# Regrouping the W' matmuls into eight bursts, and spacing the one-hot bursts of a spectral/expert mix kernel

## The chip, the cores and the metric

The kernel runs on one core of a Trainium2 chip. The metric is the device time of one execution on that core, in microseconds (us). Before the change three runs gave 765.38 us as their median, the lowest 765.37 and the highest 766.67.

A core has five engines, each with an instruction stream of its own that it works through in order: TensorE (PE, matmuls, with weight loads shown apart as PEld), VectorE (DVE), ScalarE (ACT), GpSimd (POOL) and SyncE (SP, which here issues DMA loads). They meet at semaphores: an instruction that needs another engine's result carries a wait, and everything behind it on its own engine waits with it. TensorE writes to PSUM, eight banks of 2 KB per partition (512 columns of float32); ACT and DVE read results from there.

## The reference

The output mixes two layers, token by token, for 2048 tokens of width 640:

```python
g = sigmoid((x * gate_w).sum(-1, keepdims=True))
# A: Fourier mixing, real part of a 2-d DFT by matmuls
a = einsum("bsd,ed->bse", x, dft_hid_re);  b = einsum("bsd,ed->bse", x, dft_hid_im)
A = einsum("ts,bse->bte", dft_seq_re, a) - einsum("ts,bse->bte", dft_seq_im, b)
# B: product-key experts, 32 heads, 16 x 16 keys, 256 experts
q = einsum("nd,dhc->nhc", x, w_q)
s1, s2 = q[..., :128] @ k1.T, q[..., 128:] @ k2.T       # 16 scores each
# two best of s1, two best of s2, the best two of the four sums -> expert ids and softmax gates
out_B = sum over heads and the two picks of  gate * gelu(x . u[expert]) * v[expert]
return g * A + (1 - g) * out_B
```

Two parts matter here. The scores are linear in x, so `w_q` and the keys can be multiplied first: W' = w_q x keys is a 640 x 1024 matrix (64 half-heads of 16 keys), and the scores are x times W'. And the picks of each token become a 16 x 16 table per token, built as the product of two "one-hot" matrices (rows compared with 0..15), one small matmul per token.

## The kernel before, in words

All large matmuls are float32 products in three passes (`mm3`, lines 139 to 141): both operands are split into a high part (a copy on ACT, line 134) and a low part (a subtraction on DVE or POOL, line 135). Most of them belong to the Fourier layer along the sequence. That work is cut into 152 *pieces*: each piece is one 128 x 512 block of a DFT matrix, loaded over SP into one of the `wf` tiles, split into `WS`, and multiplied with the five 128-column blocks of `X`: 15 matmuls of 128x512 that accumulate in banks 0 to 4. Everything else is laid between the pieces. The order is written out by hand: `at(n, f)` puts a function behind piece `n`, `follow(n)` calls them, and each engine's stream holds what is called in just that order. From piece 31 on, a background queue (`Pump`) also feeds in work for DVE in proportion to the TensorE time that its own account has passed.

**W'.** W' is made during the first 31 pieces. `w_q` arrives in 32 quarter blocks of 640 KB (`load_wq`, a pool of `WQB` buffers `wq`, loaded on SP). One quarter is one `w_part`: four matmuls (line 529) with 32 weight columns each, which write the four 32-partition groups of one PSUM bank, columns 0 to 319. Four quarters make one group `G` of 128 rows of W': two banks (5 and 6, from `ps_s`), two quarters added up in each. ACT copies the finished halves to `wp` (line 535). Then `w_transposes` turns the group around: five 128x128 transposes on TensorE (line 541) into bank 7 (`ps_t`), a copy on ACT (the high part, line 543) and a subtraction on DVE (the low part, line 544). `bursts` says behind which piece this happens: 16 bursts of two quarters each, behind pieces 4, 6, 8, 10, 12, 14, 16, 17, 18, 19, 20, 22, 23, 24, 25 and 27, and two that hold transposes alone. Four transposes of a group stand at the head of one burst and the fifth at the head of the next. A quarter's buffer is loaded again as soon as its matmuls are done, so the SP stream waits for TensorE there.

During the first 13 pieces `split_x` (ACT and DVE) and `gate_sum` (DVE, line 458) of the incoming rows of x stand between the same pieces; behind piece 14, `gate` runs a sigmoid on ACT.

**One-hot bursts.** From 442 to 548 us of the profiled span, `experts` handles 32 blocks of 64 tokens, two to a group. `build` makes the two one-hot matrices on DVE (lines 877 to 881). `use` issues the group's 64 matmuls of 32x32 (line 908) into bank 7, and `sums` copies the bank to `cd` on ACT (line 889) and stores it. Bank 7 is the only one for this, so the next group's matmuls wait for that copy. A group is used when two more have been built; when the buffers run short, and at `bg.drain()` behind piece 134, all that is built is used at once.

Of the kernel before, what the change touches and what calls it, by code (L numbers as in the profile page):

```python
# [8 lines left out]
F32 = mybir.dt.float32  # L9
F32R = mybir.dt.float32r  # L10
F16 = mybir.dt.float16
AF = mybir.ActivationFunctionType
# [4 lines left out]
P = 128  # L17
# [11 lines left out]
KD = D // P  # L29
# [12 lines left out]
NPC = Q1 + NT  # L42
# [58 lines left out]
def gated_mix_kernel(ctx: ExitStack, tc: tile.TileContext, xT, xn, dreT, dimT, wsre, wsim, wq, kT, uT, vv, gw, out):  # L101
    nc = tc.nc
# [9 lines left out]
    def rotate(what, n):  # L112
        turn[what] = (turn.get(what, -1) + 1) % n
        return turn[what]

    def bank(n, shape=(P, TC), dt=F32):
        return psum.tile(list(shape), dt, name=f"b{n}", tag=f"b{n}")

    def ps_s(shape=(P, TC)):
        return bank(5 + rotate("pss", 2), shape)  # L120

    def ps_t(shape, dt=F32):
        return bank(7, shape, dt)
# [25 lines left out]
    bg = Pump()  # L149
# [5 lines left out]
    WU = [big.tile([P, 2, KD, TC], F32R, name="WU", tag=f"WU{a}") for a in range(2)]  # L155
# [62 lines left out]
    def at(n, f, *args):  # L218
        then.setdefault(n, []).append(lambda: f(*args))
# [259 lines left out]
    t = ps_t([P, 512])  # L479
# [14 lines left out]
    identf = const.tile([P, P], F32)  # L494
# [16 lines left out]
    at(6, fill_rest)  # L511

    wqs, wps, wp = {}, {}, {}
    WQB = 5
    NWQ = 4 * NG

    def load_wq(m):
        if m < NWQ:
            wqs[m] = p1.tile([P, 4, HALF], F32, name="wq", bufs=WQB)
            nc.sync.dma_start(wqs[m], wq[m])  # L520

    def w_part(m):
        G, r, n = m // 4, m // 2 % 2, m % 2
        if r == 0:
            wps[G, n] = ps_s()
        ps = wps[G, n]
        w = wqs.pop(m)
        for j in range(4):
            nc.tensor.matmul(ps[32 * j:32 * j + 32, :HALF], kp[:, 8 * G // H, r, :], w[:, j], start=(r == 0),  # L529
                             stop=(r == 1))  # L530
        load_wq(m + WQB)
        if r == 1:
            if n == 0:
                wp[G] = p1.tile([P, D], F32, name="wp", bufs=1)
            nc.scalar.activation(wp[G][:, n * HALF:(n + 1) * HALF], wps.pop((G, n))[:, :HALF], AF.Copy)  # L535

    def w_transposes(G, k0, k1):
        f = wp[G]
        t = ps_t([P, 4, P])
        for k in range(k0, k1):  # L540
            nc.tensor.transpose(t[:, k - k0, :], f[:, k * P:(k + 1) * P], identf)  # L541
        h, l = (WU[G // 4][:, n, k0:k1, P * (G % 4):P * (G % 4 + 1)] for n in range(2))
        nc.scalar.activation(h, t[:, :k1 - k0], AF.Copy)  # L543
        nc.vector.tensor_sub(l, t[:, :k1 - k0], h.bitcast(F32))  # L544

    uf = {}

# [27 lines left out]
    for n in range(NT - 2):  # L575
        at(n, gate_sum, n + 2)
    for m in range(WQB):
        at(m, load_wq, m)

    bursts = [4 + m if m < 14 else 17 + (m - 14) * 10 // 16 for m in range(0, NWQ, 2)]  # L580
    n = bursts[-1]
    bursts += [n + 1, n + 2]
    for j, b in enumerate(bursts):
        if j >= 2:
            at(b, w_transposes, j // 2 - 1, *((4, KD) if j % 2 else (0, 4)))
        if 2 * j < NWQ:
            at(b, w_part, 2 * j)
            at(b, w_part, 2 * j + 1)
    n += 3
    at(n - 8, load_xT, 0)  # L590
    for k in range(KD):
# [248 lines left out]
    for p in range(NP):  # L840
        n = N0 + 5 * p + p // 2
# [20 lines left out]
    def experts():  # L862


        cd = {}

        def build(g, c, s, n, us):
            shp = [P, 16 * n, E, 4]
            pt, qt = (HOT[s // 2][:, o, s % 2:s % 2 + n].rearrange("p a (m e t) -> p (a m) e t", e=E, t=4)
                      for o in range(2))  # L870

            def row(o):
                r = ROWS[g][:, o, 8 * c:8 * (c + n), :].rearrange("p b (s t) -> p (b s) t", t=4)
                return r[:, :, None, :].to_broadcast(shp)

            wt = wtab4[:, None].to_broadcast(shp)
            nc.vector.tensor_tensor(pt, row(0), wt, op=OP.is_equal)
            yield us
            nc.vector.tensor_tensor(qt, row(1), wt, op=OP.is_equal)
            yield us  # L880
            nc.vector.tensor_tensor(pt, pt, row(2), op=OP.mult)
            yield us

        def sums(g, c, t):
            n = t.shape[1]
            if c % 4 == 0:
                cd[0] = pa.tile([P, E, 2, 4 * 8], F32, name="cd", tag="AB"[c % 8 // 4])
            o = cd[0][:, :, :, 8 * (c % 4):8 * (c % 4) + n]
            nc.scalar.activation(o.rearrange("p f t m -> p (f t) m"), t.rearrange("p m c -> p c m"), AF.Copy,  # L889
                                 scale=1.0 / GSCALE)  # L890
            c += n // 8 - 1
            if c % 4 == 3:
                w = slice(32 * (c // 4), 32 * (c // 4) + 32)
                for n in range(2):
                    nc.scalar.dma_start(gd[g, n, :, :, :, :, w].rearrange("s j e f m -> (s j e) f m"),  # L895
                                        cd[0][n::2, :, n, :])
            if c == 15:
                summed.add(g)

        def use(group):  # L900
            shape = (P, 16, E * 2)
            t = bank(7, shape)
            for a, (g, c, s) in enumerate(group):
                pt, qt = (HOT[s // 2][:, n, s % 2].rearrange("p (m c j) -> p m c j", m=16, j=2) for n in range(2))
                for m in range(16):
                    for j in range(2):
                        r = slice(64 * (m % 2) + 32 * j, 64 * (m % 2) + 32 * j + 32)
                        nc.tensor.matmul(t[r, 8 * a + m // 2, :], pt[:, m, :, j], qt[:, m, :, j], start=True,  # L908
                                         stop=True)
                free_sets.append(s)  # L910
            bg.now += 0.9 * len(group)
            bg.credit += 0.9 * len(group)
            whole = len(group) == 2 and group[0][1] % 2 == 0
            for a, (g, c, s) in enumerate(group[:1] if whole else group):
                sums(g, c, t if whole else t[:, 8 * a:8 * a + 8])
                yield 0.2

        built = deque()

        def behind(n):  # L920
            while len(built) > n:
                yield from use(built.popleft())

        while todo:
            if len(free_sets) < min(2, len(todo)):
                yield from behind(0)
            while todo[0][0] and len(rowed) < NT:
                yield -1.0
            k = min(len(todo), 2)
            group = [(*todo.popleft(), free_sets.popleft()) for n in range(k)]  # L930
            (g, c, s), odd = group[0], group[-1][2] % 2
            assert k == 1 or s % 2 == 0 and odd
            yield from build(g, c, s, k, 1.2 if k == 2 else 0.75)
            built.append(group)
            yield from behind(2)
        yield from behind(0)
# [262 lines left out]
    for n in range(N0, NPC):  # L1199
        cur = n  # L1200
        share = 0.95 if n < Q0 else 0.93
        (quad_step if Q0 <= n < Q1 else seq_piece)(n)
        follow(n)
        if n >= N1 and not HOT and len(picked) == NT:
            MID.extend(big.tile([P, 5120], F32, name="mid", tag=f"WU{a}") for a in range(2))
            for a in range(4):
                f = MID[a % 2][:, 2048 * (a // 2):2048 * (a // 2 + 1)]
                HOT[a] = f.bitcast(F16).rearrange("p (o s c) -> p o s c", o=2, s=2)
            free_sets.extend(range(8))
            mid_wf.extend(MID[a // 2][:, 4096 + TC * (a % 2):][:, :TC] for a in range(4))  # L1210
            wf_tags.extend((None, f) for f in mid_wf)
            bg.add(experts(), late=True)
        if n == RING0 - 1:
            f = big.tile([P, 2560], F32R, name="ring", tag="UU")
            mid_ring.append(f[:, :2048].rearrange("p (n a c) -> p n a c", n=2, a=2))
        if HOT and p3 is None and len(rowed) == NT:
            p2_stack.close()
            p3 = ctx.enter_context(tc.tile_pool(name="p3", bufs=1, reuse_waits="tile"))
            pools.append(p3)
            wf_tags.extend((p3, f"wf{n}") for n in (5, 6))  # L1220
        if n == NPC - 28:
            mid_wf.clear()
            for t in [t for t in wf_tags if t[0] is None]:
                wf_tags.remove(t)
        if n == NPC - 18:
            bg.drain()
        if n == NPC - 5:
            WP = p3.tile([P, 2, 2, TC], F32R, name="WP", tag="WP")
        for m in prep_split.get(n, ()):
            split_step(m)  # L1230
# [52 lines left out]
```

## Time and profile before

| | before |
|---|---|
| median of 3 runs | 765.38 us |
| profiled execution | 764.58 us |
| its span, first to last instruction | 762.7 us |
| TensorE (PE) busy | 754.8 us, 99% of the span |
| VectorE (DVE) busy | 584.7 us, 77% |
| ScalarE (ACT) busy | 303.5 us, 40% |
| GpSimd (POOL) busy | 371.8 us, 49% |
| granted TensorE clock | 1.00 in all stretches |

The profiled execution is an ordinary run: 0.8 us under the median, 1.9 us over its own span. "Busy" needs care on TensorE: matmuls overlap, so the record of a 128x512 matmul lasts 390 ns while the next one starts 230 ns after it. Time that is lost between matmuls is therefore read from the distance of their starts in the timeline, and idle time shows only what is longer than the overlap.

### The profile page before, as it was taken

How to read it: one execution, taken by the hardware profiler on the slowest of the kernel's cores; microseconds unless marked ns; L12 is line 12 of the kernel's file. 1: busy time of each engine (PE TensorE's matmuls, PEld its weight loads, DVE VectorE, ACT ScalarE, POOL GpSimd, SP SyncE). 2: the span in 40 equal slices, each digit the busy share in tenths (PEclk: the TensorE clock that was granted, in tenths of full speed). 3: DMA queues.
4: the chain of work that ended last, by engine and by line, in shares of the span. 5: the costliest groups of instructions: out<-in, count | busy, mean ns of one | idle time of the engine just before them, and what ended most of it. 6: DMA issues, size and time to landing. Idle time of an engine off the chain costs nothing.

```text
span 762.7 us, 12203 instructions
## 1 busy us (share of the span) xinstructions
PE 754.8 (99%) x4568; PEld 611.1 (80%) x4568; DVE 584.7 (77%) x667; ACT 303.5 (40%) x500; POOL 371.8 (49%) x283
## 2 busy tenths in 40 slices
PE   9999999999999999999999999999899999999997
PEld 6777667888888888888888888787788888888886
DVE  7742031377989999999999999999779999648661
ACT  5334224322323452435232464444345553543441
POOL 4523224456756494757475501642013484587253
PEclk9999999999999999999999999999999999999999
DMA  9976985636455657372944868799754785776302
GB/s 337 390 263 195 292 338 218 204 120 215 138 189 159 196 195 256 106 232 94 319 149 144 267 202 254 213 359 283 206 190 141 261 301 169 226 255 196 125 28 70
DMA packets 109629, 162.00 MB, mean 212 GB/s; under 512 B 34497, under 2 KB 49985, under 8 KB 109569
## 3 DMA queue, kind: packets, MB, share of 16 engines
q1 hardware_dynamic: 78960, 133.02, 52.8%
q10 hardware_dynamic: 26960, 15.87, 7.0%
q0 software_dynamic: 3648, 12.32, 4.7%
q8 instruction: 36, 0.59, 0.3%
q14 instruction: 25, 0.20, 0.1%
HBM read 122.90 MB, written 36.71 MB: 209 GB/s over the span
## 4 chain that ended last, share of the span: by engine, by line
PE 98%; ACT 1%; DMA 0%; ACTq 0%; issue 0%; DVE 0%; DVEq 0%
PE b L139 32%; PE b L141 31%; PE b L140 31%; PE b L529 2%; PE b L908 1%; PE b L541 1%; PE b L293 0%; DMA xr<-in_xn 0%; ACT WS L134 0%; ACT ST L303 0%; ACT L599 0%; ACT cd L889 0%; ACTq L895 0%; ACT wp L535 0%; DVE ST L1173 0%
## 5 line engine op out<-in xcount | busy, mean ns | idle before, releaser
L139 PE MATMUL b<-WS,X 128*128 128x512 f32 x520 | 205.6, 395 | 0.4 <-ACT ST L303 0.3
L140 PE MATMUL b<-WS,X 128*128 128x512 f32 x520 | 202.8, 390 | 0.0
L141 PE MATMUL b<-WS,X 128*128 128x512 f32 x520 | 202.6, 390 | 0.0
L135 POOL TENSOR_TENSOR WS<-wf,WS 128x512 fp32r<-128x512 f32 x76 | 111.5, 1473 | 154.9 <-ACT WS L134 139.3
L139 PEld LDWEIGHTS b<-WS,X 128*128 128x128 f32 x520 | 97.6, 188 | 29.7 <-issue 7.8
L134 ACT ACTIVATE WS<-wf 128x512 fp32r<-128x512 f32 x116 | 72.7, 629 | 117.6 <-PE b L141 43.7
L141 PEld LDWEIGHTS b<-WS,X 128*128 128x128 f32 x520 | 97.6, 188 | 20.8
L140 PEld LDWEIGHTS b<-WS,X 128*128 128x128 f32 x520 | 97.7, 188 | 19.4 <-DVE WS L135 0.2
L635 ACT ACTIVATE sc<-b 128x512 f32<-128x512 f32 x32 | 19.5, 608 | 118.5 <-PE b L141 109.0
L135 POOL TENSOR_TENSOR WS<-ra,WS 128x512 fp32r<-128x512 f32 x40 | 59.1, 1495 | 11.8 <-ACT WS L134 11.5
L141 PE MATMUL b<-WU,xl 128*128 128x512 f32 x160 | 62.2, 389 | 0.0
L139 PE MATMUL b<-WU,xh 128*128 128x512 f32 x160 | 62.2, 389 | 0.0
L140 PE MATMUL b<-WU,xh 128*128 128x512 f32 x160 | 62.2, 389 | 0.0
L135 POOL TENSOR_TENSOR WP<-ra,WP 128x512 fp32r<-128x512 f32 x20 | 32.4, 1635 | 47.8 <-ACT WP L134 47.8
L650 DVE TENSOR_TENSOR ew<-sc,mm 128x1024 f16<-128x1024 f32 x32 | 54.4, 1700 | 1.1
L134 ACT ACTIVATE WS<-ra 128x512 fp32r<-128x512 f32 x56 | 35.1, 631 | 49.7 <-PE b L141 31.2
L1028 DVE TENSOR_TENSOR ra<-ra 128x512 f32<-128x512 f32 x48 | 49.9, 1086 | 2.9 <-POOL WP L135 2.7
L544 DVE TENSOR_TENSOR WU<-b,WU 128x512 fp32r<-128x512 f32 (+1 forms) x16 | 7.8, 490 | 57.5 <-ACT WU L543 57.5
L648 DVE TENSOR_REDUCE mm<-sc 128x64 f32<-128x1024 f32 x32 | 38.9, 1215 | 16.4 <-ACT sc L635 15.9
L314 POOL DMA_DIRECT2D tq<-td x32 | 17.6, 552 | 56.2 <-PE b L141 56.2
L654 DVE TENSOR_REDUCE rr<-ew 128x64 f16<-128x1024 f16 x32 | 39.0, 1220 | 1.1
L652 DVE TENSOR_TENSOR ew<-ew 128x1024 f16<-128x1024 f16 x32 | 37.4, 1168 | 1.1
(190 smaller groups left out, 1547.7 us busy)
## 6 DMA issues: line engine op xcount, KB each, us to landing
wq<-in_wq SPq DMA_DIRECT2D x32, 640.0 KB, 6.9
ra<-pd SPq DMA_DIRECT2D x70, 256.0 KB, 3.9
wf<-in_wsre SPq DMA_DIRECT2D x63, 256.0 KB, 4.7
wf<-in_wsim SPq DMA_DIRECT2D x46, 256.0 KB, 3.9
sa<-in_wsim SPq DMA_DIRECT2D x32, 256.0 KB, 3.0
sd<-sa SPq DMA_DIRECT2D x32, 256.0 KB, 3.2
tq<-td POOLq DMA_DIRECT2D x32, 256.0 KB, 5.1
xf<-in_xT SPq DMA_DIRECT2D x8, 640.0 KB, 5.4
```

Of the source, the lines that this page charges most:

```text
L134: nc.scalar.activation(h, f, AF.Copy)
L135: eng.tensor_sub(l, f, h.bitcast(F32))
L139: nc.tensor.matmul(o, wh, ah, start=first, stop=False, skip_group_check=more)
L140: nc.tensor.matmul(o, wh, al, start=False, stop=False, skip_group_check=more)
L141: nc.tensor.matmul(o, wl, ah, start=False, stop=last, skip_group_check=more)
L314: nc.gpsimd.dma_start(t.bitcast(F32), td[k, :, ("s1", "s3", "a22", "s2").index(what)])
L635: nc.scalar.activation(scs[i].rearrange("p h e -> p (h e)")[:, c], ps, AF.Copy)
L648: nc.vector.tensor_reduce(m, sc, op=OP.max, axis=AX.X)
L650: nc.vector.tensor_tensor(eq, sc, m[:, :, None].to_broadcast([P, HH, E]), op=OP.is_equal)
L652: nc.vector.tensor_tensor(eq, eq, wtab, op=OP.mult)
L654: nc.vector.tensor_reduce(r, eq, op=OP.max, axis=AX.X)
L1028: nc.vector.tensor_add(take((b, o, k)) if f is not None else raw[b, o, k], raw[b, o, k] if f is None else f, raw[b, what, k])
```

## The change

Four things change. (1) W' is made in eight bursts of four quarters, behind pieces 6, 10, 13, 16, 19, 22, 25 and 27, and a ninth behind piece 28 that holds the last group's transposes alone; there are six quarter buffers in place of five. (2) All five transposes of a group stand at the head of the next burst; four go to bank 7 as before, and the fifth goes to columns 384 to 511 of the bank that the *next* group's first quarter is about to write. (3) A group of one-hot matmuls is issued only when the pump's account has moved on by 3.0 us since the one before; where buffers run short only the oldest group is used, not all; a group no longer moves that account by 0.9 us per block, and gives 0.85 us of credit per block instead of 0.9. (4) The pump is drained behind piece 137 instead of 134.

```diff
-    WQB = 5
+    WQB = 6
@@ def w_part(m):
-        if r == 0:
-            wps[G, n] = ps_s()
         ps = wps[G, n]
@@
-    def w_transposes(G, k0, k1):
+    def w_transposes(G):
         f = wp[G]
-        t = ps_t([P, 4, P])
-        for k in range(k0, k1):
-            nc.tensor.transpose(t[:, k - k0, :], f[:, k * P:(k + 1) * P], identf)
-        h, l = (WU[G // 4][:, n, k0:k1, P * (G % 4):P * (G % 4 + 1)] for n in range(2))
-        nc.scalar.activation(h, t[:, :k1 - k0], AF.Copy)
-        nc.vector.tensor_sub(l, t[:, :k1 - k0], h.bitcast(F32))
+        wps[G + 1, 0], wps[G + 1, 1] = ps_s(), ps_s()
+        for k0, k1, t in ((0, 4, ps_t([P, 4, P])), (4, KD, wps[G + 1, 0][:, None, 3 * P:])):
+            for k in range(k0, k1):
+                nc.tensor.transpose(t[:, k - k0, :], f[:, k * P:(k + 1) * P], identf)
+            h, l = (WU[G // 4][:, n, k0:k1, P * (G % 4):P * (G % 4 + 1)] for n in range(2))
+            nc.scalar.activation(h, t[:, :k1 - k0], AF.Copy)
+            nc.vector.tensor_sub(l, t[:, :k1 - k0], h.bitcast(F32))
@@
-    bursts = [4 + m if m < 14 else 17 + (m - 14) * 10 // 16 for m in range(0, NWQ, 2)]
-    n = bursts[-1]
-    bursts += [n + 1, n + 2]
-    for j, b in enumerate(bursts):
-        if j >= 2:
-            at(b, w_transposes, j // 2 - 1, *((4, KD) if j % 2 else (0, 4)))
-        if 2 * j < NWQ:
-            at(b, w_part, 2 * j)
-            at(b, w_part, 2 * j + 1)
+    bursts = [6, 10, 13, 16, 19, 22, 25, 27, 28]
+    for G, b in enumerate(bursts):
+        if G:
+            at(b, w_transposes, G - 1)
+        else:
+            wps[0, 0], wps[0, 1] = ps_s(), ps_s()
+        for m in range(4 * G, min(4 * G + 4, NWQ)):
+            at(b, w_part, m)
+    n = bursts[-1] - 1
@@ def use(group):
+            while bg.now < last[0] + 3.0:
+                yield -1.0
@@
-            bg.now += 0.9 * len(group)
-            bg.credit += 0.9 * len(group)
+            last[0] = bg.now
+            bg.credit += 0.85 * len(group)
@@
             if len(free_sets) < min(2, len(todo)):
-                yield from behind(0)
+                yield from behind(len(built) - 1)
@@
-        if n == NPC - 18:
+        if n == NPC - 15:
             bg.drain()
```

How this moves the instructions is seen best in TensorE's stream behind piece 16. The rows name the line, the tile written and the tiles read; `b5`, `b6` and `b7` are PSUM banks, `identf` and `wp` the transposes' inputs, `wq` and `kp` those of a quarter, and the bracket holds the semaphores that the instruction waits for (DMAHW: a load, the others: engines). The stream before, the burst behind piece 16 and what follows it:

```order
L541 MATMUL b7_681<-identf_144,wp_622 128x128 [waits DVE_49]
L541 MATMUL b7_681<-identf_144,wp_622 128x128 x3
L529 MATMUL b5_688<-wq_502,kp_129 32x320 [waits DMAHW6_49,PE_49]
L529 MATMUL b5_688<-wq_502,kp_129 32x320 x3
L529 MATMUL b6_695<-wq_564,kp_129 32x320 [waits DMAHW2_49,PE_49]
L529 MATMUL b6_695<-wq_564,kp_129 32x320 x3
```

And the changed stream behind the same piece, where lines 541 and 529 have become 540 and 527:

```order
L540 MATMUL b7_683<-identf_144,wp_603 128x128 [waits PE_49]
L540 MATMUL b7_683<-identf_144,wp_603 128x128 x3
L540 MATMUL b5_681<-identf_144,wp_603 128x128 [waits PE_49]
L527 MATMUL b5_681<-wq_495,kp_129 32x320 [waits DMAHW6_49,DVE_49]
L527 MATMUL b5_681<-wq_495,kp_129 32x320 x3
L527 MATMUL b6_682<-wq_503,kp_129 32x320 [waits DMAHW7_49,PE_49]
L527 MATMUL b6_682<-wq_503,kp_129 32x320 x3
L527 MATMUL b5_681<-wq_589,kp_129 32x320 [waits DMAHW4_49]
L527 MATMUL b5_681<-wq_589,kp_129 32x320 x3
L527 MATMUL b6_682<-wq_595,kp_129 32x320 [waits DMAHW5_49]
L527 MATMUL b6_682<-wq_595,kp_129 32x320 x3
```

The burst holds five transposes and sixteen quarter matmuls in place of four and eight; the fifth transpose and the first quarter write the same bank, `b5_681`, and that quarter's first matmul now waits for a DVE semaphore where it waited for TensorE's own before. The same pair of rows, with a wait for DVE on the first quarter matmul, stands at seven of the eight bursts (all but the first).

On ACT the changed stream around the same burst reads (542 and 533 are the copies to `WU` and `wp`, lines 543 and 535 before):

```order
L134 ACTIVATE WS_86<-wf_612 128x512 [waits DMAHW1_49,Pool_49]
L542 ACTIVATE WU_82<-b7_683 128x4x128 [waits PE_49]
L542 ACTIVATE WU_82<-b5_681 128x128 [waits PE_49]
L533 ACTIVATE wp_711<-b5_681 128x320 [waits DVE_49,PE_49]
L533 ACTIVATE wp_711<-b6_682 128x320 [waits PE_49]
```

The large copy and the small one follow each other directly; before, they stood a burst apart. DVE has the two subtractions in the same order (line 543 now, 544 before).

The last place is the end of the one-hot bursts. Before, in the drain behind piece 134, one group (`b7_5239`) is followed at once by the next (`b7_5307`) and by a third:

```order
L908 LDWEIGHTS mid_3573
L908 MATMUL b7_5239<-mid_3573 32x32
L908 LDWEIGHTS mid_3572 [waits DVE_49]
L908 MATMUL b7_5307<-mid_3572 32x32 [waits Activation_49]
L908 LDWEIGHTS mid_3572
```

In the changed stream the group that comes third from the end is followed by fifteen matmuls of a piece, and so is the next:

```order
L909 MATMUL b7_5246<-mid_3567 32x32
L139 MATMUL b0_4715<-ring_3623,X_255 128x512
L140 MATMUL b0_4715<-ring_3623,X_255 128x512
L141 MATMUL b0_4715<-ring_3623,X_255 128x512
L139 MATMUL b1_4800<-ring_3623,tq_3643 128x512 [waits DMASW2_49]
```

The smallest distance between two of the sixteen groups was 0 matmuls (twice) and is 15 now; all groups but the last two stand within nine matmuls of where they stood.

More of the change, by code (lines that the diff above doesn't have):

```diff
@@ L862, in experts @@
     def experts():
-        cd = {}
+        cd, last = {}, [0.0]
         def build(g, c, s, n, us):
```

## The prediction

> **What bounds the kernel now.** I read the page's head first, then the chain of waits, then the timelines of the two places that are edited. The head and the chain, with the table of waits of TensorE (PE) under them:
>
> ```profile
> span 762.7 us, 12203 instructions
> PE 754.8 (99%) x4568; PEld 611.1 (80%) x4568; DVE 584.7 (77%) x667; ACT 303.5 (40%) x500; POOL 371.8 (49%) x283
> PE 98%; ACT 1%; DMA 0%; ACTq 0%; issue 0%; DVE 0%; DVEq 0%
> PE b L908 <- ACT cd L889: 2.1, 2, 1.3
> ```
>
> PE is busy for 99% of the span and makes 98% of the chain. No other engine gives it time back: what PE gains or loses in a place, the end gains or loses. Inside the span it waits for the one-hot bank twice (2.1 us in all); the one eviction that it waits for is shown further down. All the rest has to be sought in the distance of matmul starts, which in steady state is 0.227 us.
>
> **The change part by part.** First, fewer bursts. PE around the first burst, eight quarter matmuls (two records each) between two pieces, and the records counted in steps of 0.27 us in another burst:
>
> ```profile
> 21.68 0.39 PE L141 MATMUL b<-WS,X 128*128 128x512 f32 x1
> 22.00 1.28 PE L529 MATMUL b<-wq,kp 128*32 128x320 f32 x16
> 23.21 0.50 PE L139 MATMUL b<-WS,X 128*128 128x512 f32 x1
> 23.55 0.40 PE L140 MATMUL b<-WS,X 128*128 128x512 f32 x1
> 23.79 0.40 PE L141 MATMUL b<-WS,X 128*128 128x512 f32 x1
> ...
> 73.70:73.97 0.27, 0.23 (x4) 0.16 (x8) 1.00 0.67 1
> 73.97:74.24 0.27, 0.27 (x8) 0.13 (x4) 1.00 1.57 0
> ```
>
> From 21.68 to 23.21 are 1.53 us where 0.23 would be usual, and the next two distances (0.34 and 0.24) are 0.12 too long: the burst costs 1.42 us. Four records run side by side and a new four starts every 0.27 us (in the second window eight are alive, four old and four new), so the sixteen are four steps, 1.08 us of work. The other 0.34 us is paid for going in and out, once per burst, whatever its size. Sixteen bursts become eight: 8 x 0.34 = **2.7 us saved**. The quarters themselves and the 40 transposes stay, and the transposes that now stand together cost what they did: behind piece 16 four of them took 0.53 us (73.21 to 73.74 below), one alone 0.20 (78.50 to 78.70), so 0.11 for each further one and 0.09 for the turn to the quarters. That turn replaces an entry, and I count it as nothing; so too the last burst, where five transposes alone replace four and one.
>
> Second, the new wait. This is the step on which the forecast rests. ACT copies the fifth transpose out of bank 5 and DVE subtracts from it, and only when DVE has done so may the next group's first quarter matmul write to that bank. In the instruction order it is the wait for DVE at seven bursts. The columns don't overlap (0 to 319 against 384 to 511), the bank does. Before, the same two instructions had a burst's distance and nothing waited. How long the chain takes stands in the timeline behind pieces 16 and 17 (all engines), in DVE's behind piece 8, and in ACT's and PE's at the one-hot bank:
>
> ```profile
> 73.21 0.60 PE L541 MATMUL b<-identf,wp 128*128 128x128 f32 x4
> 73.74 1.28 PE L529 MATMUL b<-wq,kp 128*32 128x320 f32 x16
> 73.84 0.60 ACT L543 ACTIVATE WU<-b 128x512 fp32r<-128x512 f32 x1 [1.76 <-PE b L541]
> 74.34 0.62 ACT L134 ACTIVATE WS<-wf 128x512 fp32r<-128x512 f32 x1
> 74.47 0.69 DVE L544 TENSOR_TENSOR WU<-b,WU 128x512 fp32r<-128x512 f32 x1 [9.30 <-ACT WU L543]
> ...
> 78.50 0.27 PE L541 MATMUL b<-identf,wp 128*128 128x128 f32 x1
> 78.70 1.28 PE L529 MATMUL b<-wq,kp 128*32 128x320 f32 x16
> 78.80 0.28 ACT L543 ACTIVATE WU<-b 128x128 fp32r<-128x128 f32 x1 [3.84 <-PE b L541]
> 79.11 0.29 DVE L544 TENSOR_TENSOR WU<-b,WU 128x128 fp32r<-128x128 f32 x1 [3.95 <-ACT WU L543]
> ...
> 41.13 0.69 DVE L544 TENSOR_TENSOR WU<-b,WU 128x512 fp32r<-128x512 f32 x1
> 41.73 1.31 DVE L135 TENSOR_TENSOR X<-xr,X 128x640 fp32r<-128x640 f32 x1
> ...
> 544.91 0.60 ACT L889 ACTIVATE cd<-b 128x512 f32<-128x512 f32 x1 [1.37 <-PE b L908]
> 545.56 0.66 PE L908 MATMUL b<-mid 128*32 128x32 f16 x64 [0.74 <-ACT cd L889]
> ```
>
> Count from the first transpose. The large copy starts at 0.63 (73.84 - 73.21), the small one 0.50 behind it (73.84 to 74.34) at 1.13. The large subtraction starts at 1.26, and DVE's next instruction follows a large one by 0.60 (41.13 to 41.73): the small subtraction starts at 1.86 (its own input would allow 1.13 + 0.31 = 1.44) and ends 0.29 later, at 2.15. From ACT's end to PE's start at the one-hot bank 0.05 us pass (545.51 to 545.56), so the quarters start at 2.20. Without the wait they would start at 0.53 + 0.11 = 0.64. PE stands still for 1.56 us per burst, **7 x 1.56 = 10.9 us lost**. What is queued behind the waiting matmul is the rest of the burst and every later piece; nothing on PE can pass it, and since PE is never waiting elsewhere, nothing gives the time back. It could hardly be less than 10.5 (1.5 each), as the five durations repeat within 0.02 us in the quiet bursts. It could be more where ACT or DVE has other work ahead. That is so while the rows of x come in, behind piece 10:
>
> ```profile
> 47.16 0.27 PE L541 MATMUL b<-identf,wp 128*128 128x128 f32 x1
> 48.32 0.74 ACT L134 ACTIVATE X<-xr 128x640 fp32r<-128x640 f32 x1 [3.68 <-DMA xr<-in_xn]
> 48.97 0.26 ACT L543 ACTIVATE WU<-b 128x128 fp32r<-128x128 f32 x1
> 50.58 0.28 DVE L544 TENSOR_TENSOR WU<-b,WU 128x128 fp32r<-128x128 f32 x1
> ```
>
> Here the subtraction starts 3.42 us after its transpose, where 0.61 is the quiet value (79.11 - 78.50): 2.8 us more, because an x row that had not landed stood ahead on ACT, and DVE had row sums to make. Bursts 10 and 13 of the changed kernel lie in that stretch: 0 to 2 x 2.8 us. I take 0.5, near the low end: in the changed order the load of that row stands behind the quarters of burst 6, not of burst 8, so that it should land some pieces earlier.
>
> A page bears on this. The Trainium skill, "PSUM — Partial Sum Buffer", section "PSUM bank collisions raise a hardware error", says that PE writing and another engine reading the same bank and partitions collide even in disjoint columns, and that access must be guarded by bank. By it the wait cannot be an oversight that costs nothing, which is the rule that speaks against this change; the trace of before never shows the two on one bank at once.
>
> Third, the wait at 69 us. ACT came late to the evictions behind piece 15, because the copies of the burst behind piece 14 and, after them, the sigmoid with its table load stood ahead:
>
> ```profile
> 66.47 1.28 ACT L599 ACT_TABLE_LOAD   x1
> 69.03 0.39 PE L141 MATMUL b<-WS,X 128*128 128x512 f32 x1
> 69.67 0.50 PE L139 MATMUL b<-WS,X 128*128 128x512 f32 x1 [0.25 <-ACT ST L303]
> 70.01 0.40 PE L140 MATMUL b<-WS,X 128*128 128x512 f32 x1
> ```
>
> 69.03 to 69.67 is 0.41 too long and the next distance 0.11. No burst stands behind piece 14 any more, so I count **0.5 us saved** (0 if ACT is late for another reason).
>
> Fourth, the one-hot bursts. One alone, and the three of the drain:
>
> ```profile
> 538.93 0.39 PE L141 MATMUL b<-WS,tq 128*128 128x512 f32 x1
> 539.25 0.67 PE L908 MATMUL b<-mid 128*32 128x32 f16 x64
> 539.85 0.50 PE L139 MATMUL b<-WS,X 128*128 128x512 f32 x1
> ...
> 543.84 0.39 PE L141 MATMUL b<-WS,tq 128*128 128x512 f32 x1
> 547.56 0.66 PE L908 MATMUL b<-mid 128*32 128x32 f16 x64 [1.34 <-ACT cd L889]
> 548.15 0.50 PE L139 MATMUL b<-WS,X 128*128 128x512 f32 x1
> ```
>
> Alone a burst takes 0.92 - 0.23 = 0.69 us, three apart 2.07; the three together take 4.31 - 0.23 = 4.08. The tails behind them (0.14 each, 0.11 of it the first distance) are two more: 0.28. **1.7 us saved**; 0 if the new spacing makes another wait. It should not: fifteen matmuls are 3.4 us, the copy of the bank takes 0.60, and in the changed order each late group's matrices are built 30 matmuls (6.8 us) ahead. The sixth buffer, the credits and the later drain cost nothing on PE. The quarter loads (6.9 us to landing, by the page) now come four at a time, 2.6 MB and three blocks of 0.26 MB in three pieces and a burst, some 15 us: 220 GB/s, and the DMA engines have moved more in this phase (the last number of a row of the windows is GB/s):
>
> ```profile
> 105.00:120.00 15.00, 15.00 (x101) 10.14 (x100) 4.59 (x7) 3.79 (x9) 3.88 (x3) 1.00 1.01 385
> ```
>
> The sum: -2.7 + 10.9 + 0.5 - 0.5 - 1.7 = **+6.5 us** on the profiled execution's 764.58, which is 771.1. That execution lies 0.8 us under the median of the runs, so the median should become 765.4 + 6.5 = **771.9 us**.
>
> **The rivals.** *The wait costs nothing* (the other side): the two instructions on bank 5 are through before PE gets to the quarters, or the chip doesn't hold them up. It is the row of the first quarter matmul that decides, from 0.64 us after the first transpose on. For it: the columns are apart, ACT and DVE are mostly idle there (in the 9.30 us before the subtraction DVE had nothing). Against it: the subtraction ends at 2.15 even on idle engines, and PE works in order. Without the stall the sum is -2.7 - 0.5 - 1.7 = -4.9, 760.5 us. 5%.
>
> *The stall is longer*: late rows of x at bursts 10 and 13, or, behind pieces 24 to 26, a late block of u ahead of the copies on ACT. The row of piece 10 is for it, the earlier loads against it. With 2.8 us at two or three bursts 5 to 8 us more, 777 to 780. 9%.
>
> *The quarters arrive late* because four loads queue up on SP behind one burst. For it: the window at 385 GB/s leaves no room for more; against it: the need is 220, and half of each burst's quarters are asked for two bursts earlier. If PE waited 1.5 us at each of four bursts: 778. 4%.
>
> *The clock falls after the stalls.* If each of the seven pauses were followed by one piece (15 x 0.227 = 3.4 us) at half speed, 24 us more: 796. Before, PE paused 1.34 us ahead of 547.56 and took 0.59 for that burst as for others, at a granted clock of 1.00: against it. 2%. The Trainium skill, "TensorE: Matmul & The Clock Gate", section "What's actually happening", has the clock halved after an idle window of about 3.4 us; a pause of 1.6 would not reach it, and the trace agrees at 1.34.
>
> **How the numbers follow.** My forecast, stall and savings as summed, has 80%; its own bounds are 10.5 to 12.5 us for the stalls with what stands ahead of them, and 3.2 to 5.3 for the savings, so +5 to +9. The rivals above it reach into the range's top, the one below it stays outside. Range 769.5 to 775.5. A measurement of this kernel tells 0.2%, 1.5 us, from no change. Faster needs the first rival (5%), no change a stall of about a third (2%), slower is the rest, 93%.
>
> **What would show it.** In the changed profile's table of waits PE should wait for DVE's subtraction into `WU` (now line 543) seven times, about 1.5 us each (the fifth transpose's record ends at 0.43 + 0.27 = 0.70 and the quarters start at 2.20), and no longer for `cd`. In the timeline the quarters should start 2.2 us after the first transpose of their burst. The wait before 69 us should be gone, and sixteen one-hot bursts should stand alone, 0.92 us from matmul to matmul. I am wrong if PE shows no wait for line 543, if the quarters' loads or ACT's late copies show up as larger than it, or if the stretch from 442 to 560 us hasn't become shorter.

## The result: 784.5 us, 2.4% slower

| | before | changed |
|---|---|---|
| median of 5 runs each, side by side | 766.62 us (765.37 to 766.73) | 784.54 us (782.62 to 785.45) |
| profiled execution, and its span | 764.58 us, 762.7 us | 783.58 us, 781.7 us |

The changed kernel takes 1.0236 times as long, 95% interval [1.0218, 1.0254]. The forecast was 771.9 us with a range up to 775.5. The sign is right; the rise is 17.9 us where 6.5 were forecast.

The changed kernel's page, its head and the head of the chain, and under them its table of what TensorE waited for (us in total, times, longest):

```profile
span 781.7 us, 12201 instructions
PE 757.5 (97%) x4568; PEld 613.7 (79%) x4568; DVE 581.9 (74%) x667; ACT 303.4 (39%) x500; POOL 379.4 (49%) x283
PE 89%; DMA 6%; DVE 2%; ACT 1%; SPq 1%; issue 0%; ACTq 0%; DVEq 0%
PE b L527 <- DVE WU L543: 18.3, 7, 4.7
```

The wait for DVE's subtraction into `WU` stands there seven times, as forecast, but it is 18.3 us long in place of 10.9. And transfers make 6% of the chain, where they made 0% before; the forecast left them to two of its rivals. TensorE's busy time grew by 2.7 us for fewer entries into bursts. That is a first sign of matmuls that ran more slowly.

Where the 19.0 us of the two profiled executions lie can be read from three marks. The first matmul of the scores starts at 145.64 us before and at 165.90 now: +20.3. From there to the first one-hot burst it is 321.61 and 321.53 us: nothing. From there to the first matmul that reads `DD`, behind all one-hot bursts, it is 144.27 and 143.08 us: -1.2. All the loss is in the W' stage.

**A quiet burst is the forecast burst.** The timeline behind piece 16 (start, duration, engine and line, operation; in brackets the idle time before, and what ended it):

```profile
81.55 0.40 PE L141 MATMUL b<-WS,X 128*128 128x512 f32 x1
81.78 0.71 PE L540 MATMUL b<-identf,wp 128*128 128x128 f32 x5
82.42 0.77 ACT L542 ACTIVATE WU<-b 128x512 fp32r<-128x512 f32 x2 [2.73 <-PE b L540]
83.06 0.89 DVE L543 TENSOR_TENSOR WU<-b,WU 128x512 fp32r<-128x512 f32 x2 [15.59 <-ACT WU L542]
84.00 2.36 PE L527 MATMUL b<-wq,kp 128*32 128x320 f32 x32 [1.50 <-DVE WU L543]
86.29 0.50 PE L139 MATMUL b<-WS,X 128*128 128x512 f32 x1
```

The quarters start 2.22 us after the first transpose (forecast 2.20). From 81.55 to 86.29 are 4.74 us where 0.23 would be usual, and the tail adds 0.15: the burst costs 4.66. The working of the forecast gives 0.34 for the entry, 2.16 of quarters, 0.53 + 0.11 for five transposes less the 0.09 of the turn and 1.56 of waiting, some 4.6. Bursts 19 and 27 cost 4.66 as well.

**Four bursts are not quiet.** The same reckoning, from the last matmul before a burst to where the starts are 0.227 us apart again, for each:

| burst behind piece | costs TensorE | of it idle | more idle than 1.50 | more than 4.66 | of it not idle |
|---|---|---|---|---|---|
| 10 | 7.85 us | 3.35 us | 1.85 us | 3.19 us | 1.34 us |
| 13 | 8.70 | 3.93 | 2.43 | 4.04 | 1.61 |
| 22 | 5.00 | 1.84 | 0.34 | 0.34 | 0.00 |
| 25 | 10.18 | 4.65 | 3.15 | 5.52 | 2.37 |
| sum | | | 7.8 | 13.1 | 5.3 |

So 13.1 us stand where the forecast had 0.5: 7.8 us of longer waits and 5.3 us in which TensorE worked, but slowly. Put into the forecast's sum (771.9 + 12.6) they give 784.5. That this meets the measured median to a tenth is partly luck: stage by stage it would be +20.8 us for W' and -1.7 for the one-hot bursts, and the traces show +20.3 and -1.2.

Where the longer wait comes from is seen at burst 10, in SP's, ACT's, DVE's and TensorE's timelines:

```profile
29.61 1.98 SPq L520 DMA_DIRECT2D wq<-in_wq  x4
...
32.32 0.82 SPq L436 DMA_DIRECT2D xr<-in_xn  x1
...
40.55 0.74 ACT L134 ACTIVATE X<-xr 128x640 fp32r<-128x640 f32 x1 [5.05 <-DMA xr<-in_xn]
...
42.05 0.74 ACT L134 ACTIVATE X<-xr 128x640 fp32r<-128x640 f32 x1 [0.24 <-DMA xr<-in_xn]
...
43.56 0.74 ACT L134 ACTIVATE X<-xr 128x640 fp32r<-128x640 f32 x1 [0.24 <-DMA xr<-in_xn]
...
45.47 0.77 ACT L542 ACTIVATE WU<-b 128x512 fp32r<-128x512 f32 x2 [1.17 <-PE b L540]
...
42.07 1.92 DVE L458 CUSTOM_DVE_ANT_0 xr<-xr,gwb 128x640 f32<-128x640 f32 x1
43.92 1.90 DVE L135 TENSOR_TENSOR X<-xr,X 128x640 fp32r<-128x640 f32 x1
...
47.97 0.88 DVE L543 TENSOR_TENSOR WU<-b,WU 128x512 fp32r<-128x512 f32 x2
...
44.83 0.71 PE L540 MATMUL b<-identf,wp 128*128 128x128 f32 x5
48.90 3.71 PE L527 MATMUL b<-wq,kp 128*32 128x320 f32 x32 [3.35 <-DVE WU L543]
```

SP asks for four quarters at once at 29.61, 2.6 MB, and only then for the row of x, at 32.32. That row lands 8.2 us later. The DMA views of 29 to 70 us of both kernels have the median to landing as the last number of a row, first the kernel before, then the changed one:

```profile
xr<-in_xn SPq DMA_DIRECT2D x5, 320.0 KB, 6.5
...
xr<-in_xn SPq DMA_DIRECT2D x5, 320.0 KB, 8.2
```

ACT waits 5.05 us for it, and two more rows land behind it at distances of 1.5 us. DVE then has its own work on three rows to do, in order. The row is there 4.3 us ahead of the transposes; it is the work of three rows, pressed together just ahead of the burst, that is not done in time. ACT's copies of the transposes are on time (0.64 us after the first transpose, as in the quiet burst); DVE's subtraction, behind the rows, starts 2.50 us after them, where 0.64 is quiet. Burst 13 is the same with a wait of 5.56 us for x. At burst 22 ACT waits 6.38 us for a block of the DFT matrix and is 0.36 us late. At burst 25 it is a block of u that is asked for 2.8 us behind four quarters, and a block of the DFT matrix behind that:

```profile
114.86 2.06 SPq L520 DMA_DIRECT2D wq<-in_wq  x4
...
117.68 0.47 SPq L549 DMA_DIRECT2D uf<-in_uT  x1
...
128.52 0.42 ACT L134 ACTIVATE UU<-uf 128x256 fp32r<-128x256 f32 x1 [7.75 <-DMA uf<-in_uT]
129.96 0.63 ACT L134 ACTIVATE WS<-wf 128x512 fp32r<-128x512 f32 x1 [1.03 <-DMA wf<-in_wsre]
130.50 0.75 ACT L542 ACTIVATE WU<-b 128x512 fp32r<-128x512 f32 x2
...
126.70 0.71 PE L540 MATMUL b<-identf,wp 128*128 128x128 f32 x5
132.06 4.50 PE L527 MATMUL b<-wq,kp 128*32 128x320 f32 x32 [4.65 <-DVE WU L543]
```

Here it is ACT that is late: the transposes ended at 127.41, the copies begin at 130.50.

The 5.3 us are the clock. Quarters that take 2.36 us in a quiet burst take 3.71 and 4.50 here. The windows view shows it (bounds, length, then PE busy; after the five engines the granted TensorE clock):

```profile
44.86:48.28 3.42, 0.68 (x6) 0.44 (x4) 3.42 (x7) 0.77 (x2) 0.28 (x1) 1.00 0.01 2
48.28:51.69 3.41, 2.79 (x24) 1.11 (x28) 0.56 (x2) 0.00 (x0) 0.00 (x0) 0.50 0.21 35
...
82.41:85.82 3.41, 1.91 (x29) 0.94 (x32) 0.89 (x2) 0.77 (x2) 0.00 (x0) 1.00 0.00 0
126.79:130.20 3.41, 0.61 (x6) 0.37 (x4) 0.43 (x1) 0.65 (x2) 0.00 (x0) 1.00 1.06 405
130.20:133.61 3.41, 1.55 (x12) 0.60 (x16) 0.89 (x2) 1.05 (x3) 1.27 (x1) 0.50 0.60 190
```

A window of 3.41 us in which TensorE was 80% or 82% idle is followed by one at half clock; one with a quiet wait in it (44% idle) is not. At burst 13 the window that is followed by half clock is 64% idle.

### The profile page after: what moved, and what is told of

It reads as the page before. It is cut to its first block, busy times and chain, and to the rows that moved or that the text cites. A ratio compares the mean times of both kernels' runs of the same rounds, so it can differ in the third digit from the quotient of the medians.

```text
span 781.7 us, 12201 instructions
## 1 busy us (share of the span) xinstructions
PE 757.5 (97%) x4568; PEld 613.7 (79%) x4568; DVE 581.9 (74%) x667; ACT 303.4 (39%) x500; POOL 379.4 (49%) x283
## 4 chain that ended last, share of the span: by engine, by line
PE 89%; DMA 6%; DVE 2%; ACT 1%; SPq 1%; issue 0%; ACTq 0%; DVEq 0%
PE b L139 28%; PE b L141 28%; PE b L140 28%; PE b L527 3%; DMA wf<-in_wsre 3%; DMA xr<-in_xn 3%; DMA mid<-in_wsim 1%; PE b L909 1%; DVE WU L543 1%; DVE xr L458 1%; DVE X L135 1%; PE b L293 0%; DVE ST L246 0%; ACT WU L542 0%; ACT WS L134 0%
## 5 line engine op out<-in xcount | busy, mean ns | idle before, releaser
L141 PEld LDWEIGHTS b<-WS,X 128*128 128x128 f32 x520 | 97.7, 188 | 20.8
L135 POOL TENSOR_TENSOR WS<-ra,WS 128x512 fp32r<-128x512 f32 x40 | 59.9, 1512 | 11.0 <-ACT WS L134 10.9
L649 DVE TENSOR_TENSOR ew<-sc,mm 128x1024 f16<-128x1024 f32 x32 | 52.7, 1646 | 1.1
L527 PE MATMUL b<-wq,kp 128*32 128x320 f32 x256 | 23.4, 515 | 18.3 <-DVE WU L543 18.3
```

The lines of the kernel that those rows point to most:

```text
L135: eng.tensor_sub(l, f, h.bitcast(F32))
L141: nc.tensor.matmul(o, wl, ah, start=False, stop=last, skip_group_check=more)
L649: nc.vector.tensor_tensor(eq, sc, m[:, :, None].to_broadcast([P, HH, E]), op=OP.is_equal)
```

## The experiments

My theory after the result: the shared bank costs its quiet wait of 1.5 us at seven bursts; what comes on top is that the quarters are asked for four at a time ahead of small loads, which makes ACT and DVE late, and that the shared bank hands their lateness to TensorE; the clock then falls where the wait is long. The rivals: the fewer, larger bursts themselves cost more than counted; the late loads hurt TensorE by themselves; the one-hot half is at fault. Each of the following was timed against the kernel before on the same chip (medians there 766.61 and 766.38 us).

### The fifth transpose in a bank of its own

Eight bursts, the changed one-hot schedule, but the fifth transpose goes to bank 7 behind the next piece, as it did before the change (`wp` gets two buffers, `wq` keeps five):

```diff
-            at(b, w_transposes, G - 1)
+            at(b + late, w_transposes, G - 1, 0, 4)
         for m in range(4 * G, min(4 * G + 4, NWQ)):
             at(b, w_part, m)
+        if G:
+            at(b + late + 1, w_transposes, G - 1, 4, KD)
```

> The changed kernel, but the fifth transpose of a group goes to bank 7 like the other four, alone behind the next piece; to make room, wp has two buffers and the quarters five again. The wait for the bank is gone, eight bursts and the loads in fours stay. Theory A (the wait for DVE on the shared bank is where all the loss enters; late rows, late blocks of u and the halved clock only lengthen it): PE waits for no WU subtraction, granted clock 1.00 throughout, 766.6 - 2.7 (bursts) - 0.5 (eviction) - 1.2 (one-hot) + 8 x 0.13 (transposes alone) = about 763. Rival B (loads four at a time cost TensorE time by themselves): over 770, with PE waiting for WS or X.

Measured: 762.37 us, ratio 0.9954 [0.9936, 0.9972]. All 22 us between this kernel and the changed one go with the place of one 128-column transpose and the buffers that this takes (the last experiment moves the transpose alone). Its waits of TensorE, and its burst 10 (ACT, DVE, TensorE):

```profile
PE b L529 <- DMA wq<-in_wq: 0.5, 1, 0.5
PE b L140 <- DVE WS L135: 0.4, 1, 0.4
```

```profile
41.05 0.74 ACT L134 ACTIVATE X<-xr 128x640 fp32r<-128x640 f32 x1 [4.62 <-DMA xr<-in_xn]
...
42.56 1.92 DVE L458 CUSTOM_DVE_ANT_0 xr<-xr,gwb 128x640 f32<-128x640 f32 x1
...
45.76 0.60 PE L541 MATMUL b<-identf,wp 128*128 128x128 f32 x4
46.29 2.36 PE L529 MATMUL b<-wq,kp 128*32 128x320 f32 x32
48.47 0.68 DVE L544 TENSOR_TENSOR WU<-b,WU 128x512 fp32r<-128x512 f32 x1
```

The row of x is as late here as in the changed kernel (4.62 us of waiting on ACT, median landing 7.9 us against 8.2), and DVE's subtraction again starts 2.7 us after the first transpose, more than twice the quiet 1.3. Nobody waits for it: TensorE goes on at 46.29, 0.53 us after the first transpose. Of the two waits that are left, the 0.4 us lie at 9 us, ahead of all bursts, and the 0.5 us are for one quarter of burst 25. So late loads and large bursts cost TensorE half a microsecond by themselves; the rest of their price comes through the bank. The first two rivals fall.

### Only the one-hot half

The kernel before with parts (3) and (4) of the change.

```diff
 def use(group):
+            while bg.now < last[0] + 3.0:
+                yield -1.0
```

> The kernel before with the one-hot part of the change alone (3.0 us of spacing, only the oldest group used, drain behind piece 137). By the starts in the two traces the change gained 1.2 us from the score stage to the end: 766.6 - 1.2 = 765.4. If the drain's pauses were all: 764.9. If a later drain only moves the waits: 766.6.

Measured: 764.14 us, ratio 0.9974 [0.9965, 0.9982]: a gain, 2.5 us by the medians. Between its first one-hot burst and the first matmul on `DD` are 142.91 us, 1.36 less than before. Its scores start 0.9 us later than before, behind the same instructions; that difference is there at 9 us already (the first matmul of line 139 starts at 9.17 and 8.24), ahead of all that was changed. So executions differ by about a microsecond at their start. The rest of the 2.5 us is taken up again under what stays open. The third rival falls.

### The shared bank, and the quarters asked for one at a time

The changed kernel; a burst's four loads are issued between the pieces up to the next burst, where the rows of x come between them. Where only three pieces lie between two bursts, two of the four still go together.

```diff
 def w_part(m):
-        load_wq(m + WQB)
@@
+        gap = (bursts[G + 1] - b) if G + 1 < len(bursts) else 1
+        for i in range(4):
+            at(b + i * (gap - 1) // 3 if G + 1 < len(bursts) else b, load_wq, 4 * G + WQB + i)
```

> The changed kernel with the bank shared as it is, but the four quarter loads that a burst frees are issued one at a time, spread over the pieces up to the next burst, behind that piece's row of x. Theory A1 (2.6 MB of quarters ahead of them make rows of x and blocks of u late, and that lengthens three of the seven waits): all seven waits about 1.5 us, no half clock, 784.5 - 13 = about 771.5. Rival C (DVE and ACT are late behind pieces 10, 13 and 25 by their own work, whatever the loads do): those three waits stay over 3 us and the time over 780.

Measured: 771.32 us, ratio 1.0064 [1.0050, 1.0079]. Thirteen of the eighteen microseconds go back by nothing but the order in which loads are asked for. The bank is still shared; its table of waits and its bursts 10 and 13:

```profile
PE b L527 <- DVE WU L542: 11.1, 7, 2.1
```

```profile
47.64 2.36 PE L527 MATMUL b<-wq,kp 128*32 128x320 f32 x32 [1.50 <-DVE WU L542]
...
63.09 3.21 PE L527 MATMUL b<-wq,kp 128*32 128x320 f32 x28 [2.10 <-DVE WU L542]
```

Burst 10 is now quiet. The median row of x still lands 7.6 us after its issue (8.2 in the changed kernel, 6.5 before); but the three rows ahead of the burst are copied by ACT at 36.39, 40.21 and 43.31, three microseconds or more apart, and DVE is through with each before the next comes. Six of the seven bursts cost about 4.65 us; only burst 13 waits 0.6 longer, and part of its quarters run at half clock. This is the kernel that the forecast described: 11.1 us of waits (forecast 10.9 and 0.5). The time of 771.3 us agrees with the forecast's 771.9 less well than it seems, as the rise is 4.7 us by the medians and 8.8 by the two spans, where 6.5 were forecast. This trace, with a half-clock window, is the slowest of the four runs; the other three, at a mean clock of 0.999 or 1.000, took 770.2 to 771.5 us.

### Keeping the clock up through the long waits

The changed kernel, with twelve idle float16 matmuls of 512 columns into bank 6 between the transposes and the quarters of bursts 10, 13 and 25. What they write is never read.

```diff
+    def fill(G):
+        for n in range(12):
+            nc.tensor.matmul(wps[G, 1], warm[:, :P], warm, start=True, stop=True)
@@
             at(b, w_transposes, G - 1)
+        if b in (10, 13, 25):
+            at(b, fill, G)
```

> The changed kernel with twelve f16 matmuls of 128x512 (about 2.6 us, into bank 6 ahead of its quarters, their result is overwritten) between transposes and quarters of the bursts behind pieces 10, 13 and 25, which fills most of their pauses of 3.4 to 4.7 us without shortening them. Theory A2 (a pause over about 3.4 us halves the clock for one or two windows of 3.4 us): granted clock 1.00, quarters of these bursts in 2.3 us in place of 3.7 and 3.3, 784.5 - 5 = about 779. Rival D (the quarters there are slow because their loads are late): they stay slow and the time stays at 784.

Measured: 783.47 us, ratio 1.0226 [1.0209, 1.0243]; the expected gain did not come. Bursts 10 and 16 of its TensorE, and the load that ACT waits for ahead of the second:

```profile
49.54 2.36 PE L527 MATMUL b<-wq,kp 128*32 128x320 f32 x32 [0.71 <-DVE WU L543]
...
80.86 0.63 ACT L134 ACTIVATE WS<-wf 128x512 fp32r<-128x512 f32 x1 [4.70 <-DMA wf<-in_wsre]
...
78.77 0.71 PE L540 MATMUL b<-identf,wp 128*128 128x128 f32 x5
82.95 0.74 PE L527 MATMUL b<-wq,kp 128*32 128x320 f32 x8 [3.48 <-DVE WU L543]
```

The twelve matmuls take 2.75 us. At bursts 10 and 13 the quarters are back at 2.36 us: on the spot the clock was the cause of the slow matmuls. The two bursts cost 3.7 us less than in the changed kernel. But burst 16, quiet in the changed kernel, now waits 3.48 us and costs 6.63, and burst 25 still falls to half clock. TensorE comes to burst 16 three microseconds sooner, but a block of the DFT matrix does not land sooner (its copy starts at 80.86, and at 79.07 in the changed kernel), and that copy stands ahead of the transposes' copies on ACT. So a microsecond won ahead of a late load is, while the bank is shared, partly waited off at the next one. The 5.3 us of slow matmuls are real in the changed kernel's account; 3.0 of them were taken away at bursts 10 and 13, and the median fell by 1.1, which the spread of the runs does not tell from nothing.

### The private bank with spread loads

The first and the third experiment together.

> The eight bursts and the spaced one-hot bursts as in the change, the fifth transpose in a bank of its own behind the next piece (as in the run with the bank alone, 762.4 us), and the four quarter loads of a burst asked for one at a time between the rows of x instead of together. By the theory that the loads' place matters only through the wait at the shared bank, taking that wait away has left nothing for it to gain: 762.0 to 762.5 us, at most the 0.9 us of waits that were left in that run's table better, 761.5. By the rival that late loads cost TensorE on their own too (the half of their price that the spread run gained back, 13 us, would then not all hang on the bank): 758 or less.

Measured: 761.60 us (760.74 to 762.66), ratio 0.9945 [0.9932, 0.9957]. By its median it is the fastest kernel of this study, 4.8 us under the one before, and 0.8 us under the private bank alone, which their intervals don't tell apart. The same spreading of the loads that was worth 13 us with the shared bank is worth at most a microsecond without it: the order of the loads matters through the bank.

### Only the W' half

The changed kernel with the one-hot bursts scheduled as before the change.

```diff
 def use(group):
-            while bg.now < last[0] + 3.0:
-                yield -1.0
```

> The changed bursts of W' with their shared bank, and the one-hot bursts scheduled as before. If the two halves of the change don't touch each other, it is slower than the changed kernel by what the one-hot half gained alone (2.5 us by its timing, 1.4 us between its first burst and the drain): 786 to 787 us. If the one-hot half gains less behind a late start, or its credits move work into the W' part, 784.5 us or less.

Measured: 784.34 us, ratio 1.0245 [1.0231, 1.0259], against 784.54 and 1.0236 for the whole change. The 786 to 787 that I expected did not come. In its trace the one-hot part is 144.42 us long, 1.3 more than in the changed kernel, so that half's gain is there; the W' stage happens to be 0.6 us shorter (the scores start at 165.32). By the medians the two halves do not add up, by the traces they nearly do, and the runs are too few to say more.

### The fifth transpose in the other of the two banks

The changed kernel; the first quarter then writes a bank that nobody holds, and TensorE comes to the wait one quarter later.

```diff
-        for k0, k1, t in ((0, 4, ps_t([P, 4, P])), (4, KD, wps[G + 1, 0][:, None, 3 * P:])):
+        for k0, k1, t in ((0, 4, ps_t([P, 4, P])), (4, KD, wps[G + 1, 1][:, None, 3 * P:])):
```

> The changed kernel with the fifth transpose in the other of the two banks that the next group's quarters fill, bank 6 in place of 5. The first quarter (four matmuls, 0.59 us at full clock) then goes to the free bank ahead of the wait, and nothing else moves. By the theory that the waiting thing is the bank, each of the seven waits becomes 0.59 us shorter, 4.1 us in all, and 780.4 us remain; the window of burst 13 (64% idle) may then no longer fall to half clock, which would give 1.7 us more, 778.7. By the rival that TensorE waits for the transposed copy itself, or for the quarters' data, nothing changes: 784.5 us.

Measured: 778.94 us (777.06 to 781.38), ratio 1.0165 [1.0150, 1.0180]: 5.6 us less than the changed kernel. Its bursts 22 (quiet) and 16 on TensorE, and the load ahead of the latter:

```profile
109.49 0.71 PE L540 MATMUL b<-identf,wp 128*128 128x128 f32 x5
110.13 0.75 PE L527 MATMUL b<-wq,kp 128*32 128x320 f32 x8
111.70 1.55 PE L527 MATMUL b<-wq,kp 128*32 128x320 f32 x20 [0.82 <-DVE WU L543]
...
79.52 0.63 ACT L134 ACTIVATE WS<-wf 128x512 fp32r<-128x512 f32 x1 [4.87 <-DMA wf<-in_wsre]
...
81.61 2.90 PE L527 MATMUL b<-wq,kp 128*32 128x320 f32 x20 [2.97 <-DVE WU L543]
```

The first quarter (eight records) runs at once, 0.64 us after the first transpose, and the wait sits behind it and is 0.7 us shorter. It is the bank that is waited for, not the data. Burst 13 lost its half clock with it (4.12 us in all, a quiet burst), as I thought it might. But burst 16 has taken on a late load and a half-clock window (7.7 us), for the reason seen in the fourth experiment: TensorE is earlier, the load isn't. Burst 25 waits longer too, 5.93 us in place of 4.65. So that the median came out near the 778.7 that I expected is luck: the quiet bursts are 0.5 us shorter (0.59 reckoned), and the late ones moved both ways. The profiled execution is the slowest of the five runs, at a mean clock of 0.990; the fastest took 777.06 us at 0.995, so the half-clock windows differ from run to run.

## Why the prediction failed, step by step

**Right.** That TensorE would wait for the bank at seven bursts, with nothing behind it that gives the time back: seven waits, 1.50 us each where the burst is quiet (forecast 1.56). The forecast of 10.9 + 0.5 us for all waits is 11.1 in the third experiment. The saving by fewer bursts and the wait at 69 us, which went with the burst behind piece 14: without the shared bank the change is 4.2 us faster than before by the medians and 3.1 by the spans; 4.9 were forecast for no wait, less about 1 us for the eight transposes that stand alone in that kernel. The one-hot half: 1.7 forecast, 1.2 to 1.4 in the traces (2.5 by its own medians). That the wait costs nothing, the rival on the other side, is false.

**The step that failed** is the term for what stands ahead on ACT and DVE: "0 to 2 x 2.8 us. I take 0.5, near the low end: in the changed order the load of that row stands behind the quarters of burst 6, not of burst 8, so that it should land some pieces earlier." It was mis-sized, 13.1 us in place of 0.5, and in three ways.

- The choice within the bounds went the wrong way. At bursts 10 and 13 the extra waits are 1.85 and 2.43 us, 4.3 in all; the bounds (0 to 5.6) held them, the value did not. The reason given looked at one row and at *when* it is asked for. That row did land ahead of the burst, by 4.3 us at burst 10. It did not look at *what is asked for just ahead of it*: behind four quarters in place of two the rows come late and close together, and DVE, with three of them in its queue, reaches the subtraction 1.85 us too late. The third experiment shows that the four loads at once were the cause: with the quarters spread burst 10 waits 1.50 us.
- The bounds named two places; there were four. Burst 25 alone (late u, 3.15 us more) was left to the rival *the stall is longer*, with 9% and 5 to 8 us. That rival is what happened, 7.8 us.
- The longer waits were not carried on to the clock. The rival *the clock falls* was priced for a fall after every one of the seven waits and set aside because a wait of 1.6 us is shorter than 3.4. It came at three of seven, where the waits were 3.35, 3.93 and 4.65 us; and the length of the wait is not the whole rule (last section). The two rivals are not apart: the first sets off the second, and together with the forecast's terms they give 784.5.

The rival *quarters arrive late* did not come: the changed kernel's TensorE waits for no `wq` load. The small loads behind the quarters were late, not the quarters.

**What stays open**: why the one-hot half gains 2.5 us by its medians and 1.4 in its trace, and nothing by medians on top of the W' half. For the first there is a likely answer in the list of runs. Of the 26 runs of the kernel before that stand beside the experiments, 16 have a mean granted clock of 0.997 and took 766.3 to 767.8 us; the other ten have 0.999 or 1.000 and took 764.8 to 765.6. All eleven runs with the one-hot half alone have 0.999 or 1.000. One window of 3.41 us at half clock lowers the mean of 765 us by 0.002. The two pauses of the drain that the change removes (0.74 and 1.34 us, 2.1 us within 2.8) are as long as the wait that cost the third experiment such a window, if they fall into one window; in the trace of the kernel before they fall into two (43% and 17% idle). Against the ten runs the gain is 1.2 us, like the trace's. No trace of a run at 0.997 is kept, so this is not shown.

## What to carry to other kernels

Before two things share a PSUM bank, list everything that the reader of that bank has queued ahead of it, loads included: the sharing turns a delay that was harmless on ACT or DVE into one of TensorE. When a load lands depends on what its queue was asked for just before; batching large loads makes the small ones behind them late (8.2 us in place of 6.5 for a row of x) and brings them in a bunch, and that is harmless only as long as nobody that matters stands behind them. And a wait of TensorE has two prices: its length, and a half-clock window where it leaves enough of one window of 3.41 us idle (59% here; 53% was not enough).

## What the hardware showed that was not expected

**The clock gate judges a fixed window, not a pause.** In all the traces the half-clock stretches of the W' stage are 3.41 us long or twice that, and in a trace they start on one grid (48.28, 68.76 and 130.20 in the changed kernel: 6 and 18 times 3.413 apart). What decides is how idle TensorE was within the grid's window before. The windows that lie nearest to each other, from the runs with the idle matmuls and with only the W' half:

```profile
77.89:81.30 3.41, 1.59 (x10) 1.14 (x8) 0.00 (x0) 0.44 (x1) 0.00 (x0) 1.00 0.54 45
81.30:84.72 3.42, 1.77 (x28) 0.93 (x32) 0.89 (x2) 0.84 (x3) 1.27 (x1) 1.00 0.02 0
```

```profile
125.42:128.83 3.41, 1.41 (x9) 0.98 (x7) 0.00 (x0) 0.14 (x1) 0.00 (x0) 1.00 1.05 402
128.83:132.24 3.41, 0.09 (x4) 0.09 (x8) 1.31 (x3) 1.56 (x4) 1.27 (x1) 0.50 0.67 234
```

A pause of 3.48 us that the grid cuts into windows of 53% and 48% idle leaves the clock alone; a window that is 59% idle is followed by half clock. No window at full clock of the W' stage in the nine traces contradicts this; between 53% and 59% none lies. In the third experiment a wait of only 2.10 us was enough, as all of it fell into one window:

```profile
60.50:63.92 3.42, 1.32 (x17) 0.67 (x19) 2.54 (x6) 0.77 (x2) 0.30 (x1) 1.00 0.03 10
63.92:67.33 3.41, 3.41 (x25) 1.37 (x18) 0.00 (x0) 0.89 (x3) 0.00 (x0) 0.50 0.63 202
```

The Trainium skill, "TensorE: Matmul & The Clock Gate", section "What's actually happening", says that the window is 3413 ns and free-running, and the traces agree; it speaks of an idle window, and here 59% of one was enough. I had read that section as a rule on pauses of 3.4 us.

**Two instructions of DVE took twice as long beside POOL.** In the rows of burst 10 they took 1.92 and 1.90 us where the same forms take 0.81, while POOL was at work on `WS`, from 41.89 to 43.30 and from 43.39 to 45.14. Both began while an instruction of POOL ran, and each ended 0.7 us behind it. The instruction of DVE before them, which had begun at 41.33, ahead of POOL's, took 0.82. That lengthened the queue ahead of the subtraction by 2.2 us, more than the 1.85 us that burst 10 waits above the quiet 1.50: by this estimate the burst would have been quiet without POOL's work at that moment, even with the late rows. The Trainium skill, "SBUF — State Buffer", section "Who interferes with whom", has the two engines share a port by an exclusive lock; the rows agree with that, and no run here tested it.
